# Half-row transposes, a shorter decoding, softmax sums dealt to 128 partitions and a third value buffer in a fused attention and two-MLP kernel

## The chip, the cores and the metric

One core of a Trainium2 chip runs the whole program. The metric is the device time of one execution in microseconds (us); lower is better. PE is TensorE (PEld its weight loads), DVE is VectorE, ACT is ScalarE, POOL is GpSimd and SP is SyncE, which issues most of the transfers.

## What is computed

Attention with a tanh cap over 2 batches of 12 heads (448 tokens, 64 columns per head), then an MLP with a sigmoid gate, then an MLP with RMS norm and a SiLU gate. The change touches attention alone.

```python
scores = scale * np.matmul(q, k.transpose(0, 1, 3, 2))
scores = cap * np.tanh(scores / cap)
attn = np.exp(scores - max)
attn = attn / (np.sum(attn, axis=-1, keepdims=True) + 1e-09)
return np.matmul(attn, v)
x = _moe_ref(x, w_in, w_out)                  # h * sigmoid(1.702 h) between two products
return _moe2_ref(x, w_gate, w_val, w_out, rms_g)
```

The kernel leaves out the subtraction of the maximum, since the cap bounds the scores.

## The kernel before

**Precision.** Products that need it are made of three products of halves: an operand is split into a rounded part (float32r) and the rest. Weights are split too: a weight tile of 128 x 768 is decoded from its bits by a row of ScalarE passes (`square`, `sign`, `mask`, then `high_part`) and VectorE passes (`mid`, `top`, `low`, then `low_part`).

**Attention.** The 24 heads are worked on as 12 pairs, numbered 0 to 11. A loop of 13 iterations (numbered p = 0 to 12) writes the instructions of all engines by hand, and every engine keeps the order in which they are written. Iteration p holds, for TensorE: the scores of pair p for the key chunks 1 and 2 (`scores`, L298, twelve products), the scores of the last 64 keys (`scores_last`, L308), the transposes of q and k of pair p+2 (`turn`, L251), the first scores of pair p+1 (L298, six products), the output product of pair p-1 (`outputs`, L336) and its sums of exponentials (`sums`, L368). ScalarE does the tanh and the exponential of each chunk (`exps`, L320 and L321). VectorE splits the transposes (`split_kq`, L271 and L272), adds exponentials of the chunks (`add_two` L352, `add_third` L355), copies the output product out of PSUM (L344), normalizes an older pair (`normal`: L398, L410 and L417), takes the reciprocal of the sums (L373), and does its share of decoding.

**The way of the reciprocals.** The sums of a pair stand on four partitions of a PSUM tile. For pairs 0 to 8 the reciprocal goes to DRAM (`keep_recips`, L378, 3.5 KB, named recs<-rs) and comes back spread over 128 partitions (`spread`, L383, 224 KB, named r<-recs). Both are issued by POOL, whose queue also holds the two small copies of keys for `scores_last` (L274). In iteration p POOL issues, behind those copies, `spread(p-2)` and then `keep_recips(p-1)`; `spread` waits until the DRAM tile has landed. VectorE multiplies with it in `normal(p-4)`. The last three pairs use a TensorE product (L389) in place of the way through DRAM, and its operand is the reciprocal on VectorE (L373).

**The end of attention.** In iteration 12 VectorE does `normal(8)`, the reciprocal of pair 11, `normal(10)` and then `normal(11)`. The first MLP starts with two column blocks for batch 0; between the first and the second TensorE makes the spreading product of pair 11 (L389), and the third block needs every pair of batch 1 normalized.

**PSUM.** `scores_last`, `outputs` and `sums` share two buffers, so a product waits until VectorE or ScalarE has read the one before it.

Of the kernel before, what the change touches and what calls it, by code (L numbers as in the profile page):

```python
# [18 lines left out]
def attn_moe_kernel(  # L19
# [23 lines left out]
    NC = 3  # L43
# [75 lines left out]
    def square(w):  # L119
# [5 lines left out]
        nc.scalar.activation(out=f(d), in_=f(r[:, :, 1]), func=AF.Square, scale=2.0 ** 15)  # L125
# [51 lines left out]
    def attention():  # L177
        with ExitStack() as actx:
# [15 lines left out]
            vns = [ap_.tile([128, 4, NC, D], F32, name=f"vn{i}", bufs=1) for i in range(2)]  # L194
            ves = [ap_.tile([128, 2, 2, D], F32, name=f"ve{i}", bufs=1) for i in range(2)]
# [36 lines left out]
            def load_v(g):  # L232
# [3 lines left out]
                    out=vns[g % 2][:, 0:2 * n].rearrange("p h c d -> p h (c d)"),  # L236
                    in_=v[b, h0:h0 + 2 * n, 0:NC * 128].rearrange("h (p c) d -> p h (c d)", c=NC),
                )
                for e in range(2):
                    nc.sync.dma_start(  # L240
                        out=ves[g % 2][half[e], 0:n, e], in_=rows(v, p0, n, NC * 128, S)[:, e:2 * n:2]
# [4 lines left out]
            def turn(p):  # L246
# [6 lines left out]
                if p:  # L253
                    t = ps_t.tile([128, 2, 512], F32, tag="t", name="t").rearrange("p a s -> p (a s)")
                    for c in range(2 * NC + 1):
                        flip(t[:, c * 128:(c + 1) * 128], c)
# [9 lines left out]
            def split_kq(p):  # L266
                t = turned.pop(p)
                if p:
                    x = ap_.tile([128, 2, 2 * S], F32R, tag="x", name="x")
                    xs[p] = [[x[:, a, j * S:(j + 1) * S] for j in range(2)] for a in range(2)]  # L270
                    nc.vector.tensor_copy(x[:, 0], t[:, 0:2 * S])  # L271
                    nc.vector.tensor_tensor(out=x[:, 1], in0=t[:, 0:2 * S], in1=f(x[:, 0]), op=ALU.subtract)  # L272
# [54 lines left out]
            def outputs(p, cs=range(NC + 1)):  # L327
# [5 lines left out]
                for c in cs:  # L333
                    for e in range(2):
                        w = vns[g % 2][:, 2 * i + e, c] if c < NC else ves[g % 2][:, i, e]
# [6 lines left out]
                zt[p] = zrp.tile([128, S], F32, tag="z", name="z", bufs=5)  # L342
# [99 lines left out]
            def warm_up(times):  # L442
# [6 lines left out]
                3: [(square, 0)], 4: [(sign, 0)], 5: [(mask, 0)], 6: [(square, 1)], 7: [(sign, 1)],  # L449
                8: [(mask, 1)], 9: [(high_part, 0)], 11: [(high_part, 1)],  # L450
# [3 lines left out]
                6: [(mid, 0)], 7: [(top, 0)], 8: [(low, 0)], 9: [(mid, 1)],  # L454
# [17 lines left out]
            for p in range(NPR + 1):  # L472
# [32 lines left out]
                if p >= 4:  # L505
                    normal(p - 4)
# [5 lines left out]
                if p >= 2 and p - 2 < NPR - 3:  # L512
                    spread(p - 2)
# [398 lines left out]
```

## Time and profile before

| | us |
|---|---|
| median of 3 runs (608.05 to 608.64) | 608.14 |
| the profiled execution | 608.84 |
| its span from the first to the last instruction | 607.0 |
| busy: TensorE, VectorE, ScalarE, GpSimd | 599.3, 456.5, 398.2, 71.8 |

The granted TensorE clock is full speed throughout the span. A busy TensorE says little, since the records of products that are queued behind one another run together. What a stage costs is read from the starts of the same instruction in successive iterations. The chain of waits, followed back from the last instruction, is 87% TensorE and 8% transfers; a part of attention and its end are in the hands of the transfers issued by POOL.

Attention takes the first 108 us or so of the span, the rest are the two MLPs, in which TensorE runs without a pause.

### The profile page before, as it was taken

What the parts mean: (1) busy time and instruction counts of PE and PEld (TensorE: products, weight loads), DVE (VectorE), ACT (ScalarE), POOL (GpSimd) and SP (SyncE); (2) the same over time, 40 slices, a digit from 0 to 9 for tenths busy, and PEclk for the clock granted to TensorE, in tenths of its full rate; (3) what the DMA queues carried; (4) which work ended last, traced back from release to release, by engine and by line L of the source; (5) the groups of instructions that cost most, each with busy time, mean ns of one, the idle gap of its engine ahead of it and who ended that gap; (6) DMA issues with size and microseconds to landing.
All of it is one profiled execution on the core that took longest, in us unless ns stands there. A gap on an engine that the chain in (4) does not pass through costs nothing.

```text
span 607.0 us, 8472 instructions
## 1 busy us (share of the span) xinstructions
PE 599.3 (99%) x3328; PEld 510.2 (84%) x3328; DVE 456.5 (75%) x556; ACT 398.2 (66%) x533; POOL 71.8 (12%) x95
## 2 busy tenths in 40 slices
PE   8999999999999999999999999999999999999997
PEld 5555553789988899988888888899989999999997
DVE  2889998699774635667788899995588897588842
ACT  5999998499874547777676657684555483366400
POOL 4232321000000000000032202200022200122100
PEclk9999999999999999999999999999999999999999
DMA  6676232064443332333333333433133342233012
GB/s 151 157 208 175 62 108 85 7 198 139 133 155 105 104 105 59 120 127 111 105 104 105 105 104 105 130 131 105 56 119 124 118 131 84 100 105 104 1 77 105
DMA packets 78567, 67.16 MB, mean 111 GB/s; under 512 B 29440, under 2 KB 75830, under 8 KB 78528
## 3 DMA queue, kind: packets, MB, share of 16 engines
q1 hardware_dynamic: 74064, 64.27, 34.5%
q0 software_dynamic: 3664, 2.16, 1.3%
q8 instruction: 26, 0.43, 0.3%
q10 hardware_dynamic: 800, 0.20, 0.1%
q14 instruction: 13, 0.11, 0.1%
HBM read 63.80 MB, written 2.78 MB: 110 GB/s over the span
## 4 chain that ended last, share of the span: by engine, by line
PE 87%; DMA 8%; issue 2%; DVE 1%; POOL 1%; ACT 0%; POOLq 0%; DVEq 0%
PE b L598 22%; PE b L597 22%; PE b L596 22%; PE b L806 14%; DMA recs<-rs 7%; PE s L298 2%; DMA r<-recs 2%; PE v L336 1%; PE t L251 1%; POOL r L383 1%; PE v L444 1%; PE v L308 1%; PE v L368 0%; DVE x L271 0%; DVE x L272 0%
## 5 line engine op out<-in xcount | busy, mean ns | idle before, releaser
L598 PE MATMUL b<-x,ring 128*128 128x512 f32 (+1 forms) x480 | 174.3, 363 | 0.0
L597 PE MATMUL b<-x,ring 128*128 128x512 f32 (+1 forms) x480 | 174.1, 363 | 0.0
L596 PE MATMUL b<-x,ring 128*128 128x512 f32 (+1 forms) x480 | 174.0, 362 | 0.0
L596 PEld LDWEIGHTS b<-x,ring 128*128 128x128 f32 x480 | 90.1, 188 | 10.4 <-issue 0.3
L597 PEld LDWEIGHTS b<-x,ring 128*128 128x128 f32 x480 | 90.1, 188 | 9.9
L598 PEld LDWEIGHTS b<-x,ring 128*128 128x128 f32 x480 | 90.1, 188 | 9.4
L137 DVE SCALAR_TENSOR_TENSOR dec<-raw,dec 128x768 uint32<-128x768 uint32 x68 | 69.6, 1024 | 24.7 <-ACT dec L133 23.4
L806 PE MATMUL b<-ring,uA 128*128 128x384 f32 x504 | 87.8, 334 | 0.0
L806 PEld LDWEIGHTS b<-ring,uA 128*128 128x128 f32 x504 | 87.4, 188 | 0.0
L143 DVE SCALAR_TENSOR_TENSOR dec<-raw,dec 128x768 uint32<-128x768 uint32 x68 | 73.1, 1075 | 1.1
L158 ACT ACTIVATE ring<-dec 128x768 fp32r<-128x768 f32 x68 | 56.7, 834 | 21.7 <-DVE dec L149 13.5
L163 DVE TENSOR_TENSOR ring<-dec,ring 128x768 fp32r<-128x768 f32 x68 | 66.8, 984 | 4.5 <-ACT ring L158 4.5
L598 PE MATMUL b<-g,ring 128*128 128x384 f32 (+1 forms) x192 | 70.0, 365 | 0.0
L597 PE MATMUL b<-g,ring 128*128 128x384 f32 (+1 forms) x192 | 69.9, 364 | 0.0
L596 PE MATMUL b<-g,ring 128*128 128x384 f32 (+1 forms) x192 | 69.6, 362 | 0.0
L149 DVE SCALAR_TENSOR_TENSOR dec<-raw,dec 128x768 uint32<-128x768 uint32 x68 | 64.9, 954 | 1.5
L129 ACT ACTIVATE dec<-dec,edge 128x768 f32<-128x768 f32 x68 | 63.4, 932 | 1.0
L125 ACT ACTIVATE dec<-raw 128x768 f32<-128x768 f32 x68 | 61.0, 897 | 0.6 <-DVE ring L163 0.5
L133 ACT ACTIVATE dec<-dec 128x768 f32<-128x768 f32 x68 | 57.3, 842 | 1.5
L774 POOL TENSOR_TENSOR a<-a,gg 128x512 f32<-128x512 f32 (+1 forms) x18 | 29.6, 1646 | 188.6 <-DVE gg L767 188.6
L777 ACT ACTIVATE uA<-a 128x512 fp32r<-128x512 f32 (+1 forms) x24 | 13.9, 578 | 46.3 <-POOL a L774 34.5
L628 DVE TENSOR_TENSOR g<-gg,g 128x384 fp32r<-128x384 f32 (+1 forms) x32 | 20.0, 626 | 25.9 <-ACT g L625 25.7
(104 smaller groups left out, 685.3 us busy)
## 6 DMA issues: line engine op xcount, KB each, us to landing
raw<-in_moe_w_out SPq DMA_DIRECT2D x20, 768.0 KB, 4.2
raw<-in_moe_w_in SPq DMA_DIRECT2D x16, 768.0 KB, 4.6
raw<-in_moe_w_gate SPq DMA_DIRECT2D x12, 768.0 KB, 4.2
raw<-in_moe_w_val SPq DMA_DIRECT2D x12, 768.0 KB, 4.2
raw<-in_moe_w_out SPq DMA_DIRECT2D x8, 512.0 KB, 3.8
out<-oacc SPq DMA_DIRECT2D x6, 384.0 KB, 2.3
raw<-in_moe_w_out SPq DMA_DIRECT2D x8, 256.0 KB, 3.5
r<-recs POOLq DMA_DIRECT2D x9, 224.0 KB, 7.9
```

What stands on the lines that cost most here:

```text
L125: nc.scalar.activation(out=f(d), in_=f(r[:, :, 1]), func=AF.Square, scale=2.0 ** 15)
L129: nc.scalar.activation(out=f(d), in_=f(d), func=AF.Sign, bias=edge)
L133: nc.scalar.activation(out=f(d), in_=f(d), func=AF.Relu, scale=2.0 - 2.0 ** -23)
L137: nc.vector.scalar_tensor_tensor(out=d, in0=hi, scalar=3, in1=d, op0=ALU.logical_shift_left, op1=ALU.bitwise_and)
L143: nc.vector.scalar_tensor_tensor(out=d, in0=hi, scalar=0xC0000000, in1=d, op0=ALU.bitwise_and, op1=ALU.bitwise_or)
L149: nc.vector.scalar_tensor_tensor(out=d, in0=lo, scalar=29, in1=d, op0=ALU.logical_shift_right, op1=ALU.bitwise_or)
L158: nc.scalar.activation(out=t[:, 0], in_=f(dec_t[w][0]), func=AF.Copy)
L163: nc.vector.tensor_tensor(out=t[:, 1], in0=f(d), in1=f(t[:, 0]), op=ALU.subtract)
L596: nc.tensor.matmul(out=wide(o, b), lhsT=w0, rhs=x0, start=first, stop=False)
L597: nc.tensor.matmul(out=wide(o, b), lhsT=w0, rhs=x1, start=False, stop=False)
L598: nc.tensor.matmul(out=wide(o, b), lhsT=w1, rhs=x0, start=False, stop=last)
L806: nc.tensor.matmul(out=os_[t][n][:, 0:HW], lhsT=uA[xi][:, i, tok], rhs=w[:, wi, n * HW:(n + 1) * HW], start=(i == 0 and xi == 0 and wi == ...
```

## The change

- `turn`: each of the seven transposes of 128 rows becomes two of 64 rows, one for each half of the partitions, into two PSUM banks; `split_kq` reads and writes in matching pieces of 64 columns.
- `sums`: for every pair the third chunk's exponentials are added on VectorE (`add_third` now also for pairs 6 to 11), so TensorE's eight products on that chunk go. For pairs 0 to 8 VectorE copies the sums out of PSUM in place of taking the reciprocal.
- `deal` (new): a transfer issued by POOL lays the 4 x 224 sums out as 128 x 7. `keep_recips` takes the reciprocal of the 7 columns on VectorE and stores them to DRAM. Iteration p now has `spread(p-3)`, `keep_recips(p-2)`, `normal(p-5)`, `sums(p-1)` and `deal(p-1)`. At the end iteration 10 has `normal(5)` and `normal(6)`, iteration 11 `normal(7)` and `normal(9)`, iteration 12 `normal(8)` and `normal(10)`.
- Decoding of the first two weight tiles: the ScalarE passes `square`, `sign` and `mask` become one (`size`); VectorE does `clip` and `field` in place of `mid`.
- Three value buffers in place of two.

```diff
-            vns = [ap_.tile([128, 4, NC, D], F32, name=f"vn{i}", bufs=1) for i in range(2)]
+            vns = [ap_.tile([128, 4, NC, D], F32, name=f"vn{i}", bufs=1) for i in range(3)]
...
-                        flip(t[:, c * 128:(c + 1) * 128], c)
+                        for a in range(2):
+                            nc.tensor.transpose(
+                                t[:, a, c * 64:(c + 1) * 64],
+                                raws[g % 2][half[a], c, 2 * i:2 * i + 2].rearrange("p h d -> p (h d)"),
+                                ident[half[a], half[a]],
+                            )
...
-                    nc.vector.tensor_copy(x[:, 0], t[:, 0:2 * S])
+                    flat = t[:, :, 0:S].rearrange("p a (c n) -> p a c n", n=64)
+                    high, low = [x[:, m].rearrange("p (c a n) -> p a c n", a=2, n=64) for m in range(2)]
+                    nc.vector.tensor_copy(high, flat)
...
-                for c in (1, NC) if p < NP else (1, 2, NC):
+                for c in (1, NC):
...
-                nc.vector.reciprocal(out=nr[p], in_=ps[:, 0:SH])
+                if p < NPR - 3:
+                    nc.vector.tensor_copy(nr[p], ps[:, 0:SH])
+                else:
+                    nc.vector.reciprocal(out=nr[p], in_=ps[:, 0:SH])
+
+            def deal(p):
+                rs = nr[p]
+                nr[p] = zrp.tile([128, SH // 32], F32, tag="rc", name="rc", bufs=2)
+                nc.gpsimd.dma_start(out=nr[p], in_=rs[0:128:32].rearrange("n (k c) -> n k c", k=32))
 
             def keep_recips(p):
-                rs = nr[p]
+                rc = nr[p]
+                nc.vector.reciprocal(out=rc, in_=rc)
                 nr[p] = dram.tile([4, SH], F32, tag="recs", name="recs", bufs=3)
-                nc.gpsimd.dma_start(out=nr[p], in_=rs[0:128:32])
+                nc.gpsimd.dma_start(out=nr[p].rearrange("n (k c) -> (n k) c", k=32), in_=rc)
...
-                3: [(square, 0)], 4: [(sign, 0)], 5: [(mask, 0)], 6: [(square, 1)], 7: [(sign, 1)],
-                8: [(mask, 1)], 9: [(high_part, 0)], 11: [(high_part, 1)],
+                5: [(size, 0)], 7: [(size, 1)], 9: [(high_part, 0)], 11: [(high_part, 1)],
...
-                6: [(mid, 0)], 7: [(top, 0)], 8: [(low, 0)], 9: [(mid, 1)],
+                6: [(clip, 0), (field, 0)], 7: [(top, 0)], 8: [(low, 0)], 9: [(clip, 1), (field, 1)],
...
-                if p >= 4:
+                if p >= 3 and p - 3 < NPR - 3:
+                    spread(p - 3)
+                if p >= 2 and p - 2 < NPR - 3:
+                    keep_recips(p - 2)
+                if 5 <= p < NPR - 1:
+                    normal(p - 5)
+                if NPR - 2 <= p:
                     normal(p - 4)
...
-                if p >= 2 and p - 2 < NPR - 3:
-                    spread(p - 2)
                 if p >= 1:
                     sums(p - 1)
                     if p - 1 < NPR - 3:
-                        keep_recips(p - 1)
+                        deal(p - 1)
...
-                if p < NP:
+                if p < NPR:
                     add_third(p)
```

POOL's queue, from the copies of keys in iteration 4 to those of iteration 5 and the `spread` behind them, before (kb: keys for `scores_last`; r<-recs is `spread`; recs<-rs is `keep_recips`):

```order
L274 CAST kb0_108<-x_578 64x2x64 [waits DVE_49,PE_49,Pool_49]
L274 CAST kb0_108<-x_578 64x2x64 [waits Pool_49]
L383 DMA r_606<-recs_525 128x1x448 [waits DMASW6_49]
L378 DMA recs_619<-rs_617 4x224 [waits DMASW0_49,DVE_49]
L274 CAST kb1_109<-x_666 64x2x64 [waits DVE_49,PE_49,Pool_49]
L274 CAST kb1_109<-x_666 64x2x64 [waits Pool_49]
L383 DMA r_694<-recs_619 128x1x448 [waits DMASW3_49,DMASW1_49,DMASW0_49]
```

And the same stretch after (rc<-rs is `deal`; the DRAM tile that is written, 553 and 653, is the one that the next `spread` waits for):

```order
L298 CAST kb0_110<-x_625 64x2x64 [waits DVE_49,PE_49,Pool_49]
L298 CAST kb0_110<-x_625 64x2x64 [waits Pool_49]
L416 DMA r_650<-recs_553 128x1x448 [waits DMASW6_49,DMASW0_49]
L411 DMA recs_653<-rc_566 128x7 [waits DMASW1_49,DVE_49]
L405 DMA rc_666<-rs_664 128x1x7 [waits DMASW2_49,DVE_49]
L298 CAST kb1_111<-x_721 64x2x64 [waits DVE_49,PE_49,Pool_49]
L298 CAST kb1_111<-x_721 64x2x64 [waits Pool_49]
L416 DMA r_746<-recs_653 128x1x448 [waits DMASW1_49]
```

Each iteration has a third transfer, behind the other two, and each `spread` belongs to a pair one older than before.

VectorE in iteration 10, from the copy of the output product of pair 9 (L344) on, before:

```order
L344 COPY z_1120<-v_1111 128x448 [waits PE_49]
L398 TENSOR_TENSOR z_867<-z_867,r_959 128x448 [waits DMASW7_49]
L410 CAST x0_66<-z_867 128x448 [waits DVE_49]
L417 TENSOR_TENSOR x1_67<-z_867,x0_66 128x448 [waits DVE_49]
L373 RECIPROCAL rs_1140<-v_1127 128x224 [waits DMASW4_49,PE_49]
L143 SCALAR_TENSOR_TENSOR dec_738<-raw_445,dec_738 128x768
```

And after (rc is the dealt tile of pair 8, z_844 and z_943 are pairs 5 and 6, L379 is `add_third(10)`):

```order
L368 COPY z_1210<-v_1201 128x448 [waits PE_49]
L409 RECIPROCAL rc_1157<-rc_1157 128x7 [waits DMASW5_49,DMASW1_49]
L431 TENSOR_TENSOR z_844<-z_844,r_1038 128x448 [waits DMASW4_49]
L443 CAST x0_66<-z_844 128x448 [waits DVE_49]
L450 TENSOR_TENSOR x1_67<-z_844,x0_66 128x448 [waits DVE_49]
L431 TENSOR_TENSOR z_943<-z_943,r_1138 128x448 [waits DMASW7_49]
L443 CAST x0_66<-z_943 128x448 [waits DVE_49]
L450 TENSOR_TENSOR x1_67<-z_943,x0_66 128x448 [waits DVE_49]
L400 RECIPROCAL rs_1232<-v_1223 128x224 [waits PE_49]
L379 TENSOR_TENSOR ts_1199<-ts_1199,tt_1182 128x896 [waits Activation_49]
L160 SCALAR_TENSOR_TENSOR dec_893<-raw_478,dec_893 128x768 [waits DMAHW7_49]
```

The reciprocal of 7 columns, which waits for a transfer (DMASW5 is the `deal` of pair 8), a second normalization and `add_third` have come into this stretch.

## Rows read from the trace of the kernel before

**Rows 1.** Chain that ended last: start us, us, what; the end of attention

```profile
92.54 6.29 DMA recs<-rs
98.83 0.29 issue
99.12 9.49 DMA r<-recs
...
111.97 0.61 PE b L389 x8
```

**Rows 2.** Timeline of PE, first scores of iterations 3 to 7 and 10: start, us

```profile
30.36 1.57 PE L298 MATMUL s<-x 64*128 64x448 f32 x12
...
38.31 1.58 PE L298 MATMUL s<-x 64*128 64x448 f32 x12
...
46.27 1.58 PE L298 MATMUL s<-x 64*128 64x448 f32 x12
...
54.91 1.48 PE L298 MATMUL s<-x 64*128 64x448 f32 x12
...
62.75 1.49 PE L298 MATMUL s<-x 64*128 64x448 f32 x12
...
87.46 1.48 PE L298 MATMUL s<-x 64*128 64x448 f32 x12
```

**Rows 3.** Timeline of PE's weight loads in iteration 4; [idle before <-releaser]

```profile
38.31 0.50 PEld L298 LDWEIGHTS s<-x 64*128 64x128 f32 x6 [0.36 <-issue]
...
39.81 0.50 PEld L308 LDWEIGHTS v<-x,kb 128*128 128x128 f32 x3 [0.30 <-issue]
40.33 0.89 PEld L251 LDWEIGHTS t<-ident,kq 128*128 128x128 f32 x7
```

**Rows 4.** Groups of DVE, 22 to 108 us: count | busy us, mean ns | idle

```profile
L373 DVE RECIPROCAL rs<-v 128x224 f32<-128x224 f32 x11 | 17.1, 1551 | 0.3 <-PE v L368 0.3
...
L355 DVE TENSOR_TENSOR ts<-ts,tt 128x896 f32<-128x896 f32 x5 | 5.2, 1042 | 0.1
...
L410 DVE CAST x<-z 128x448 fp32r<-128x448 f32 x9 | 3.5, 394 | 0.3
...
L137 DVE SCALAR_TENSOR_TENSOR dec<-raw,dec 128x768 uint32<-128x768 uint32 x2 | 1.8, 896 | 0.0
```

**Rows 5.** Timeline of POOL, issues of transfers and copies of keys

```profile
30.75 0.82 POOL L383 DMA_DIRECT2D r<-recs  x1
...
35.98 1.33 POOL L274 CAST kb<-x 64x128 fp32r<-64x128 f32 x2 [2.81 <-DVE x L272]
...
50.75 0.80 POOL L383 DMA_DIRECT2D r<-recs  x1 [5.47 <-DMA recs<-rs]
...
59.16 0.80 POOL L383 DMA_DIRECT2D r<-recs  x1 [5.40 <-DMA recs<-rs]
...
82.23 0.80 POOL L383 DMA_DIRECT2D r<-recs  x1 [4.23 <-DMA recs<-rs]
...
99.12 0.80 POOL L383 DMA_DIRECT2D r<-recs  x1 [6.01 <-DMA recs<-rs]
```

**Rows 6.** DMA issues, 22 to 112 us: count, KB each, median us to landing

```profile
r<-recs POOLq DMA_DIRECT2D x9, 224.0 KB, 7.9
...
recs<-rs POOLq DMA_DIRECT2D x9, 3.5 KB, 7.2
```

**Rows 7.** Timeline of DVE: the shortest reciprocal, iterations 10 to 12, and after

```profile
5.02 0.16 DVE L467 RECIPROCAL tsc<-capt 128x1 f32<-128x1 f32 x1 [3.50 <-DMA capt<-in_cap]
...
93.75 0.62 DVE L344 COPY z<-v 128x448 f32<-128x448 f32 x1 [1.90 <-PE v L336]
94.29 0.61 DVE L398 TENSOR_TENSOR z<-z,r 128x448 f32<-128x448 f32 x1
...
108.64 0.63 DVE L398 TENSOR_TENSOR z<-z,r 128x448 f32<-128x448 f32 x1 [1.45 <-DMA r<-recs]
...
110.27 1.55 DVE L373 RECIPROCAL rs<-v 128x224 f32<-128x224 f32 x1
...
113.30 0.68 DVE L405 TENSOR_TENSOR z<-z,b 128x224 f32<-128x224 f32 x2
```

More of the change, by code (lines that the diff above doesn't have):

```diff
@@ L117, in attn_moe_kernel, with open_ @@
     dec_t, done = {}, set()
-    def square(w):
+    def open_(w):
         load_to(w)
@@ L123, in square, with size, clip, field @@
         dec_t[w] = (d, r[:, :, 0], r[:, :, 1])
-        nc.scalar.activation(out=f(d), in_=f(r[:, :, 1]), func=AF.Square, scale=2.0 ** 15)
+        return dec_t[w]
+    def size(w):
+        d, lo, hi = open_(w)
+        nc.scalar.activation(out=f(d), in_=f(hi), func=AF.Abs)
+    def clip(w):
+        d = dec_t[w][0]
+        nc.vector.tensor_scalar(out=f(d), in0=f(d), scalar1=2.0 ** -15, scalar2=None, op0=ALU.max)
+    def field(w):
+        d = dec_t[w][0]
+        nc.vector.tensor_scalar(
+            out=d, in0=d, scalar1=3, scalar2=0x3FFFFFFF, op0=ALU.logical_shift_left, op1=ALU.bitwise_and
+        )
+    def square(w):
+        d, lo, hi = open_(w)
+        nc.scalar.activation(out=f(d), in_=f(hi), func=AF.Square, scale=2.0 ** 15)
     def sign(w):
@@ L191, in attention @@
             raws = [ap_.tile([128, 2 * NC + 1, 4, D], F32, name=f"kq{i}", bufs=1) for i in range(2)]
-            vns = [ap_.tile([128, 4, NC, D], F32, name=f"vn{i}", bufs=1) for i in range(2)]
-            ves = [ap_.tile([128, 2, 2, D], F32, name=f"ve{i}", bufs=1) for i in range(2)]
+            vns = [ap_.tile([128, 4, NC, D], F32, name=f"vn{i}", bufs=1) for i in range(3)]
+            ves = [ap_.tile([128, 2, 2, D], F32, name=f"ve{i}", bufs=1) for i in range(3)]
             kbs = [ap_.tile([128, 2, 128], F32R, name=f"kb{i}", bufs=1) for i in range(2)]
@@ L235, in load_v @@
                 nc.sync.dma_start(
-                    out=vns[g % 2][:, 0:2 * n].rearrange("p h c d -> p h (c d)"),
+                    out=vns[g % 3][:, 0:2 * n].rearrange("p h c d -> p h (c d)"),
                     in_=v[b, h0:h0 + 2 * n, 0:NC * 128].rearrange("h (p c) d -> p h (c d)", c=NC),
@@ L240, in load_v @@
                     nc.sync.dma_start(
-                        out=ves[g % 2][half[e], 0:n, e], in_=rows(v, p0, n, NC * 128, S)[:, e:2 * n:2]
+                        out=ves[g % 3][half[e], 0:n, e], in_=rows(v, p0, n, NC * 128, S)[:, e:2 * n:2]
                     )
@@ L253, in turn @@
                 if p:
-                    t = ps_t.tile([128, 2, 512], F32, tag="t", name="t").rearrange("p a s -> p (a s)")
+                    t = ps_t.tile([128, 2, 512], F32, tag="t", name="t")
                     for c in range(2 * NC + 1):
-                        flip(t[:, c * 128:(c + 1) * 128], c)
+                        for a in range(2):
[3 more added lines that the diff above has]
+                                ident[half[a], half[a]],
+                            )
                 else:
@@ L341, in outputs @@
                     return
-                zt[p] = zrp.tile([128, S], F32, tag="z", name="z", bufs=5)
+                zt[p] = zrp.tile([128, S], F32, tag="z", name="z", bufs=6)
                 if p < NPR - 1:
```

4 lines of the change are left out of this document (2 added, 2 removed).

## The prediction, made before the changed kernel ran

> **What bounds the kernel now.** I read the chain of waits first. In the MLPs it is TensorE without a break; the edits leave those alone, so their time moves only with their start. At the end of attention the chain leaves TensorE: it runs through POOL's transfers, the store of the reciprocals (recs) and their spreading (r), up to 108.61, and comes back by VectorE to TensorE's product L389 at 111.97 [rows 1]. So two things are to be priced: how fast attention runs, and when its last reciprocals arrive.
>
> In the middle TensorE sets the pace. The same scores start at 54.91 and 62.75: 7.84 us for an iteration in which it waits for nobody. Iterations 3 and 4 take 7.95 and 7.96 (a ScalarE decoding pass in each), iteration 5 takes 8.64, and 7 to 9 take 24.71 together, 8.24 each [rows 2].
>
> Beside it runs a loop of transfers. An r moves 224 KB and takes 7.9 us to land; recs moves 3.5 KB and still takes 7.2, since it is issued right behind an r and lands right after it [rows 6, 1]. The next r waits for that recs. So the r follow each other at the pace of their own latency: 30.75, two links of 10.0 to 50.75, one of 8.4 to 59.16, three of 7.7 to 82.23, two of 8.45 to 99.12. Each issue was released by recs [rows 5]. The last r lands at 108.6, VectorE has waited 1.45 us for it, and only then comes the reciprocal of pair 11 (110.27) that L389 needs [rows 7, 1].
>
> **The change part by part.** *Sums with add_third.* The third chunk's products made iterations 7 to 9 longer: 24.71 - 3 x 7.84 = 1.2 us go on TensorE.
>
> *ScalarE's passes and the value buffers.* What iterations 3 and 4 take over 7.84 goes with the passes (.2), and what iteration 5 takes over it goes with the earlier value load and the later mask (.8): the bound from below is that the wait stays (0), but a load that no longer waits for its buffer is ahead of need by more than the .8. With the 1.2 above iteration 10 starts 2.2 us earlier, at 85.3. One more buffer costs two memsets on POOL before TensorE's first product; they lie under the warm-up.
>
> *Transposes.* A pair of half loads starts as one: six loads of 64 rows take .50 us, as three of 128 rows do [rows 3]. So seven pairs of half loads should take about what seven whole ones take (.89), and I price them at 0. The bounds: half (-.4 per iteration), if 64 columns count for half of 128; and double (+.8, the .89 without the tail of its last load), if the two loads follow one another. The switch from whole rows to half rows moves from behind the transposes to before them, which cancels.
>
> A rule speaks against the edit. The Trainium skill ("TensorE: Matmul & The Clock Gate", section "LDWEIGHTS (loading the stationary operand)") says that a load takes as long for 32 rows as for 128, only the columns count. By that rule alone, 14 loads in place of 7, the edit costs the double bound; the row on six half loads shows that the two halves load side by side, which the section does not speak of, and I follow the row.
>
> *VectorE.* For pairs 0 to 8 the reciprocal of 1.55 us becomes a copy of 128 x 224 out of PSUM, near the .34 that one of the two L405 takes, and a reciprocal of 7 columns, between the .16 of one column and the .39 of L410; I take .2 [rows 4, 7]. That is -1.0 each. add_third comes in six times more, 1.04 each, 1.0 with the overlap of neighbours. Clip and field in place of mid (.90): a one-operand pass lies between .39 (L410, 448 columns) and .90 (L137, 768); at .6 each they add .3 to iterations 6 and 9, at .9 they add .9 [rows 4]. The strided split keeps its count of elements; I price it at 0. In iterations 6 to 9 this balances; VectorE has some 7.5 us of work in 7.84.
>
> *The loop of transfers, with a third transfer.* POOL's first r comes behind the keys of iteration 3, which end at 35.98 + 1.33 = 37.3, where it was at 30.75 [rows 5]: the loop starts 6.6 us later and has the same nine links, since each r still waits for a recs issued behind the r before it. Only the kinds of links change: one of 10.0 in place of two (the first weight tiles are in by then), two of 8.4, three of 7.5 (7.7 is their average with a decoding load in it). So the r of pair 6 is issued at 37.3 + 10.0 + 16.8 + 22.5 = 86.6 and lands 8.1 later (8.45 less the .3 from landing to issue), at 94.7. Bounds: six links of 7.7 and a landing of 7.4 give 90.9; the links of before (82.23 - 30.75) and 8.1 give 96.9.
>
> Now the new wait. The deal of a pair is issued behind an r too, and VectorE waits for it in order: in iteration 10 the reciprocal of pair 8 stands behind r(6). Queued behind it on VectorE are normal(5), normal(6), the reciprocal of pair 9 (which frees a PSUM buffer for TensorE's outputs of pair 10), add_third, decoding, and so all that leads to L389. How long a deal takes with no r ahead of it no row shows. The Trainium skill ("DMA: Bandwidth & Descriptors", section "Why a DMA increments its semaphore by 16 and not by 1") says that for transfers issued by GpSimd all 16 engines post, whatever the shape; by that the deal is done only when the r ahead of it is, and the 7.2 us of recs agree. Without it there would be no wait and the sum would be that of the first rival.
>
> *The end of attention.* Without the wait, the copy at 93.75 would start at 91.5 and VectorE would be at the reciprocal of pair 8 at 92.1; with it, at 94.7. Before, VectorE went from 94.29 to the reciprocal at 110.27 in 15.98 us, 1.45 of them waiting: 14.5 of work [rows 7]. After, the same stretch has a second normalization (1.63, from 108.64 to 110.27), two add_third (2.0) and the small reciprocal (.2): 18.35. So the last reciprocal starts at 94.7 + 18.35 = 113.05. It also needs r(8): two more links of 8.45 and 8.1 give 86.6 + 16.9 + 8.1 = 111.6, and 1.63 of normal(8) 113.2. Both say 113.2 against 110.27: **+3.0 us**. What TensorE gains before is used up by waiting at the products of pair 10 and at L389; in this stretch it has less work than VectorE. From L389 on nothing changes.
>
> The profiled execution took 608.84 (span 607.0 and 1.84 around it), which becomes 611.8; on the median of 608.14 it is **611.1**.
>
> **Rivals.** (1) *The deals are in time.* If the links are all like the fastest, r(6) lands at 90.9 and VectorE is there at 92.1: the last reciprocal starts at 110.5, +.2 us, 608.3. It decides at the landing of r(6), before or after 92. For it: the links from 59.16 to 82.23. Against: the loads of q, k, v and weights that stretched links to 8.4 and 10 are still there.
>
> (2) *Faster: half-row transposes cost half.* Then iterations 3 to 9 each lose what VectorE's 7.5 us allow, .3, together 2.1; iteration 10's copy is done at 90.0, and if r(6) has landed by then (the shortest loop of all), the last reciprocal starts at 108.4: -1.9 us, 606.2. Both conditions are needed, since VectorE's 18.35 us follow whichever is later. For it: 64 columns are half of 128. Against: loads, not columns, seem to set the pace of a transpose, and the loop starts 6.6 us late.
>
> (3) *Slower still.* Half loads one after the other add .8 to seven iterations, less what the wait for the deal hides: 92.1 + 5.6 = 97.7, the last reciprocal at 116.0, +5.8, 613.9. The skill's rule on columns is this case. A loop with all the links of before gives 96.9 + 18.35 = 115.25, +5.0, 613.1.
>
> **How the numbers follow.** The forecast, a wait of 1 to 4 us for the transfers at the end, gets .52; rival 1 .22; rival 2 .13; rival 3 .13. About .2% or 1.2 us is what a measurement of this kernel can tell from no change. Faster .13 is rival 2, the same .22 is rival 1, slower .65 the rest. The range goes from 607.6 (rival 1 with cheaper new passes on VectorE) to 614.0 (rival 3's price); it leaves out most of rival 2 and the dearest of rival 3.
>
> **What would show it.** Right: the first r at about 37.3, nine r with links of 7.4 to 10; a wait of VectorE for rc<-rs in iterations 4 to 10, the longest in iteration 10; TensorE's iterations of 7.9 or so and its stalls at the outputs of pair 10 and at L389; the last reciprocal near 113. Wrong: recs landing well before the r ahead of it, links under 7; no wait of VectorE for the dealt tile; a transpose at half or double its present price; the new passes on VectorE far from .6.

## The result, and the profile after

The changed kernel takes 611.62 us (median of 6 runs, 611.1 to 614.24) where the kernel before took 608.1 in the same session (607.68 to 608.85). The ratio is 1.0059, with a 95% interval of 1.0041 to 1.0078: **3.5 us slower**, where 3.0 was forecast. The profiled execution has a span of 610.8 us, against 607.0 before.

| us from the start of the span | before | after | difference |
|---|---|---|---|
| scores of iteration 10 begin on TensorE | 87.46 | 87.05 | -0.41 |
| VectorE's z copy of iteration 10 | 93.75 | 94.87 | +1.12 |
| reciprocal of pair 11, the last one | 110.27 | 114.00 | +3.73 |
| product that spreads it (L389, now L422) | 111.97 | 115.70 | +3.73 |
| end of the span | 607.0 | 610.8 | +3.8 |

So all of the loss is made in attention, 1.1 us of it up to the copy of iteration 10 and 2.6 in the three iterations behind it; the MLPs only start later. That is read with the timelines, which are shown by engine here, each against its group of before.

TensorE's first scores, iterations 4 to 10 (start, us), against [rows 2], and behind the last of them the scores of the last 64 keys:

```profile
37.40 1.49 PE L322 MATMUL s<-x 64*128 64x448 f32 x12
...
44.92 1.49 PE L322 MATMUL s<-x 64*128 64x448 f32 x12
...
52.44 1.49 PE L322 MATMUL s<-x 64*128 64x448 f32 x12
...
61.01 1.48 PE L322 MATMUL s<-x 64*128 64x448 f32 x12
...
69.63 1.50 PE L322 MATMUL s<-x 64*128 64x448 f32 x12
...
77.46 1.49 PE L322 MATMUL s<-x 64*128 64x448 f32 x12
...
87.05 2.53 PE L322 MATMUL s<-x 64*128 64x448 f32 x12
89.51 1.35 PE L332 MATMUL v<-x,kb 128*128 128x448 f32 x3
```

Iterations 4 and 5 take 7.52 us, better than the 7.84 that was TensorE's pace before. Then come 8.57, 8.62, 7.83 and 9.59. What TensorE had gained by 52.44 (2.5 us, since the same scores stood at 54.91) is nearly all gone by 87.05. The reason stands on VectorE, whose timeline is cut here to the small reciprocals that wait for a deal, to iteration 10 and to the last reciprocal ([idle before <-releaser]), against [rows 7]:

```profile
46.50 0.20 DVE L409 RECIPROCAL rc<-rc 128x7 f32<-128x7 f32 x1 [1.70 <-DMA rc<-rs]
...
54.82 0.20 DVE L409 RECIPROCAL rc<-rc 128x7 f32<-128x7 f32 x1 [2.50 <-DMA rc<-rs]
...
63.44 0.20 DVE L409 RECIPROCAL rc<-rc 128x7 f32<-128x7 f32 x1 [1.88 <-DMA rc<-rs]
...
86.92 0.20 DVE L409 RECIPROCAL rc<-rc 128x7 f32<-128x7 f32 x1 [0.53 <-DMA rc<-rs]
...
94.87 0.62 DVE L368 COPY z<-v 128x448 f32<-128x448 f32 x1 [2.80 <-PE v L360]
95.41 0.19 DVE L409 RECIPROCAL rc<-rc 128x7 f32<-128x7 f32 x1
...
114.00 1.55 DVE L400 RECIPROCAL rs<-v 128x224 f32<-128x224 f32 x1
```

VectorE waits for the deals of iterations 4, 5, 6 and 9, 6.6 us together. From the second half of iteration 4 on it runs behind TensorE and TensorE follows it. The chain of waits shows how the lag reaches iteration 10 (start us, us, what):

```profile
48.13 6.67 DMA rc<-rs
...
57.20 6.15 DMA rc<-rs
...
81.86 0.88 DVE dec L166
...
82.77 0.84 ACT ring L175
...
85.58 0.53 ACT tl L344
...
86.16 0.96 PE v L392 x16
87.12 2.46 PE s L322 x12
```

ScalarE's decoding pass L175 stands between two of its attention passes and waits for VectorE's L166, which is late; so its passes for pair 9 are late. One of them (`tl`, L344) reads the scores of the last 64 keys and so frees the PSUM buffer that TensorE's sums need, and they wait for it until 86.16. What that does to the clock is in the busy table by stretches:

```profile
core 0: us, PE busy (x) PEld busy (x) DVE busy (x) ACT busy (x) POOL busy (x), PEclk, DMA share, GB/s
79.50:87.00 7.50, 5.50 (x54) 2.40 (x52) 6.89 (x10) 5.12 (x7) 2.81 (x6) 1.00 0.49 121
87.00:91.00 4.00, 4.00 (x21) 2.80 (x19) 3.90 (x9) 3.93 (x5) 1.98 (x3) 0.57 0.62 177
91.00:100.00 9.00, 6.95 (x53) 3.29 (x51) 6.07 (x11) 6.87 (x8) 1.54 (x2) 1.00 0.13 37
100.00:104.40 4.40, 4.08 (x14) 1.40 (x16) 4.37 (x6) 1.30 (x2) 0.81 (x1) 0.61 0.13 22
```

PEclk is the granted clock: 0.57 and 0.61 in two stretches of 4 us, so for the greater part the 1.2 GHz level, and 2.4 GHz around them. Each follows a long wait of TensorE (2.0 us of it for ScalarE before 86.16, 2.4 for VectorE before 100.32). A long wait alone doesn't bring such a fall: in a_spread16 and a_nodeal (below) TensorE waits 2.38 us before 95.92 and 2.39 before 51.08, and the granted clock is 1.00 behind both. The scores at 87.05 took 2.53 where the six rows above them took 1.5, and those of the last 64 keys took 1.35 where they take 0.84 to 0.88 in the iterations above: 1.5 us together, all of it on the path to the copy at 94.87, and just what lies between -0.41 and +1.12 in the table. The other stretch costs little, because VectorE waits only 0.38 us for TensorE behind it. The fall of the clock is not what makes the loss: of the six executions one had a mean granted clock of 1.000, and it took 611.1 us.

Last, POOL's issues, against [rows 5]:

```profile
37.10 0.81 POOL L416 DMA_DIRECT2D r<-recs  x1 [0.51 <-DMA recs<-rc]
...
46.77 0.80 POOL L416 DMA_DIRECT2D r<-recs  x1 [2.66 <-DMA recs<-rc]
...
86.91 0.80 POOL L416 DMA_DIRECT2D r<-recs  x1 [0.55 <-DMA recs<-rc]
```

and the price of an r in the page's list of DMA issues (count, KB each, median us to landing), against [rows 6]:

```profile
r<-recs POOLq DMA_DIRECT2D x9, 224.0 KB, 7.5
```

The loop is the forecast one: first r at 37.1 (37.3 forecast), then links of 9.7, 8.1, 8.5, 7.8, 7.6 and 8.0 to the r of pair 6 at 86.9 (86.6 forecast).

Two of the later issues, at 71.24 and 78.87, show no wait for recs: the key copies ahead of them ended at 71.2 and 78.7, up to 0.3 us after the recs had landed.

Why an r is so slow stands in the posts of the 16 DMA engines, which the trace has for each transfer of POOL's queue (an engine posts when it is through with its share). For the stretch behind 78.87 (times of the first post, the 14th, and the last two):

```
issued  transfer    1st    14th   15th   16th
78.87   r<-recs     81.2   81.5   86.0   86.4
79.66   recs<-rc    81.5   81.7   86.3   86.6
81.17   rc<-rs      83.0   83.4   86.5   86.8
```

Fourteen engines are through with the r 2.6 us after its issue; two carry its 224 KB and need 7.5. The recs and the deal issued behind it are done on fourteen engines too; their last two posts come 0.2 us after one another's, right behind those of the r, so they wait for the same two. The Trainium skill ("DMA: Bandwidth & Descriptors", section "Why a DMA increments its semaphore by 16 and not by 1") has the reason: a transfer is split over the largest number of engines up to 16 that divides the slowest dimension of both of its sides. The source of r is [2, 64, 448], and 2 is what it gets; the posts agree.

### The profile page after: what moved, and what is told of

It is laid out like the page before. It is cut to its first block, busy times and chain, and to the rows that moved or that the text cites. A ratio compares the mean times of both kernels' runs of the same rounds, so it can differ in the third digit from the quotient of the medians.

```text
span 610.8 us, 8565 instructions
## 1 busy us (share of the span) xinstructions
PE 596.2 (98%) x3357; PEld 505.5 (83%) x3357; DVE 453.7 (74%) x573; ACT 395.1 (65%) x529; POOL 79.5 (13%) x106
## 4 chain that ended last, share of the span: by engine, by line
PE 85%; DVE 6%; DMA 4%; ACT 3%; issue 1%; POOL 0%; DVEq 0%; POOLq 0%
PE b L634 22%; PE b L633 22%; PE b L632 22%; PE b L842 14%; DMA recs<-rc 2%; DMA rc<-rs 2%; PE v L360 2%; ACT tt L345 1%; ACT tt L344 1%; PE s L322 1%; DVE x L450 1%; DVE rs L400 1%; DVE z L431 1%; PE v L477 1%; DVE ts L379 1%
## 5 line engine op out<-in xcount | busy, mean ns | idle before, releaser
L175 ACT ACTIVATE ring<-dec 128x768 fp32r<-128x768 f32 x68 | 56.7, 834 | 26.6 <-DVE dec L166 18.4
L166 DVE SCALAR_TENSOR_TENSOR dec<-raw,dec 128x768 uint32<-128x768 uint32 x68 | 64.9, 955 | 1.4
L146 ACT ACTIVATE dec<-dec,edge 128x768 f32<-128x768 f32 x66 | 61.5, 932 | 1.0
L142 ACT ACTIVATE dec<-raw 128x768 f32<-128x768 f32 x66 | 59.3, 898 | 0.6 <-DVE ring L180 0.5
L150 ACT ACTIVATE dec<-dec 128x768 f32<-128x768 f32 x66 | 55.6, 842 | 1.5
L734 POOL TENSOR_TENSOR sqs<-sqs,sq 128x384 f32<-128x384 f32 (+1 forms) x10 | 11.7, 1166 | 235.4 <-ACT sq L730 235.4
```

What stands on the lines that cost most here:

```text
L142: nc.scalar.activation(out=f(d), in_=f(hi), func=AF.Square, scale=2.0 ** 15)
L146: nc.scalar.activation(out=f(d), in_=f(d), func=AF.Sign, bias=edge)
L150: nc.scalar.activation(out=f(d), in_=f(d), func=AF.Relu, scale=2.0 - 2.0 ** -23)
L166: nc.vector.scalar_tensor_tensor(out=d, in0=lo, scalar=29, in1=d, op0=ALU.logical_shift_right, op1=ALU.bitwise_or)
L175: nc.scalar.activation(out=t[:, 0], in_=f(dec_t[w][0]), func=AF.Copy)
```

## The experiments

Two theories stand against each other. **Transfers:** the deals lie behind an r that two engines carry, VectorE waits for them, and that costs the time. **Work:** VectorE's longer list in the last iterations costs it, and the waits fill slack. Ratios are to the kernel before in the same session, with 95% intervals. In the session of the changed kernel it took 608.1 us; in that of a_spread16, b_spread16, b_half and a_nodeal 608.8; in that of a_dealsp, a_third6, a_spread16_n4 and a_spread16_n4_t10 608.5; and in that of the other four 610.1. Times of different sessions are compared only as closely as these agree.

### r on all engines, in both kernels

```
-                nc.gpsimd.dma_start(out=nr[p], in_=d.unsqueeze(1).to_broadcast([2, 64, S]))
+                for e in range(2):
+                    nc.gpsimd.dma_start(out=nr[p][half[e]], in_=d[e:e + 1].to_broadcast([64, S]))
```

In the changed kernel, a_spread16:

> The changed kernel with one edit: the spreading r<-recs is issued as two transfers of 64 rows instead of one of [2, 64, 448]. In the changed kernel's trace 14 of the 16 DMA engines have posted 2.4 us after an r is issued and two post 6.9 us after, so one r is carried by two engines; its rows of 64 should be dealt to all. Theory (the deals and recs are late because they lie behind an r that two engines carry): each r lands 2.5 to 3.5 us after its issue, the deals land within 4 us, VectorE's waits for rc<-rs (6.6 us in all, the 2.8 us wait for TensorE at 94.87 that follows from them) go, iterations stay at 7.5 to 7.7, the last reciprocal starts at 108.5 to 109.5 instead of 114.0: 606 to 607.2. Rival (the longer work of VectorE in the last three iterations is what costs, the waits only fill slack): the last reciprocal stays within 1 us of 114.0: 610.5 to 612.

Measured: 608.03 us (607.59 to 608.55, 10 runs), ratio 0.9984 (0.9974 to 0.9993), 3.6 us less than the changed kernel's 611.62 of the other session. Its DMA issues, 22 to 112 us (count, KB each, median us to landing), and then its timelines of TensorE (iteration 10) and VectorE:

```profile
r<-recs POOLq DMA_DIRECT2D x18, 112.0 KB, 3.1
vn<-in_v SPq DMA_DIRECT2D x4, 384.0 KB, 4.8
...
rc<-rs POOLq DMA_DIRECT2D x9, 3.5 KB, 2.9
```

```profile
83.72 1.58 PE L322 MATMUL s<-x 64*128 64x448 f32 x12
...
91.01 0.19 DVE L409 RECIPROCAL rc<-rc 128x7 f32<-128x7 f32 x1
...
109.12 1.55 DVE L400 RECIPROCAL rs<-v 128x224 f32<-128x224 f32 x1
```

An r lands in 3.1 us in place of 7.5, a deal in 2.9, and there is no wait for a deal any more. Iterations 4 to 8 take 7.52 each, and the last reciprocal starts 4.9 us earlier. The whole loss is gone with the two engines: transfers, not work, in this sense. But from the deal in iteration 10 to the last reciprocal VectorE still needs 18.1 us. The time came 0.8 us above the range that was expected, though the last reciprocal came where it was expected: the profiled execution took 607.71, 5.0 less than the 612.67 of the changed kernel's, and the expectation had taken the 4.9 off the median.

In the kernel before, b_spread16:

> The kernel before with that edit alone: r issued as two transfers of 64 rows. Theory: r lands about 3 us after its issue where it took 7 to 9.5, recs no longer lands behind it, the links of the loop are no longer 7.7 to 10 us but the pace of the iterations; VectorE's wait of 1.45 us for r at 108.6 goes, the last reciprocal comes at about 108.8 instead of 110.27: 606.0 to 607.0. Rival (TensorE's own pace sets the end and the transfer only seems last): within 0.5 us of 608.1. Rival (a spread is slow through its latency, not through its two engines): latency of r stays above 6 us and nothing changes.

Measured: 607.32 us (607.18 to 608.0, 7 runs), ratio 0.9972 (0.9961 to 0.9983). The two rivals fall (an r lands in 3.4 us), and the gain is 1.4 to 1.7 us, by the medians and by the ratio. The time is 0.3 above the theory's range; the gain is the 1.1 to 2.1 that this range meant under 608.1. The last reciprocal:

```profile
107.90 1.55 DVE L373 RECIPROCAL rs<-v 128x224 f32<-128x224 f32 x1
```

It comes 2.4 us before that of [rows 7], without a wait. TensorE's product follows only at 110.46, 1.5 us earlier than before: by then TensorE itself is busy.

### The half-row transposes alone

The kernel before with the transposes and the strided split of the change, b_half:

> The kernel before with the half-row transposes and the strided split alone. The changed kernel's trace has 14 half transposes in 0.43 us, where 7 whole ones took 0.65; an iteration is 7.52 where it was 7.84. Theory (in the kernel before the loop of transfers sets the end, TensorE does not): the iterations shorten by 0.3, iteration 10 begins near 85 instead of 87.46, but the r keep their own links, the last one lands at 107.8 to 108.6, VectorE waits about 3 us for it: 607.3 to 608.3. Rival (TensorE's pace sets the end): minus 2 to 2.7 us, 605.4 to 606.1.

Measured: 609.54 us (607.36 to 613.57, 10 runs), ratio 1.0017 (0.9992 to 1.0042): no gain, and 1.2 us above the theory's range. VectorE at the end (start, us, [idle before <-releaser]):

```profile
108.77 0.62 DVE L405 TENSOR_TENSOR z<-z,r 128x448 f32<-128x448 f32 x1 [1.75 <-DMA r<-recs]
...
110.40 1.55 DVE L380 RECIPROCAL rs<-v 128x224 f32<-128x224 f32 x1
```

The last r lands when it did, whatever TensorE does: before the change, the loop of transfers set the end. That was the theory, and the rival (a gain of 2 us or more) falls. One part of the theory is wrong: iterations 3 and 4 still take 7.96 and 7.97, since ScalarE's passes hold them, iteration 5 takes 8.96 with a wait of 1.30 for its values, and 7 to 9 take 8.0 each, so iteration 10 begins at 87.20 and not near 85. Half rows, with that r on all engines, b_half_spread16:

> The kernel before with r in two transfers of 64 rows (607.3 by itself) and the half-row transposes. Theory (TensorE has 0.31 us less per iteration, but ScalarE holds iterations 3 and 4 at 7.97, and VectorE with some 7.9 us of work holds 7 to 9): iteration 10 begins at 85.3 to 86.0 instead of 86.58, 606.2 to 607.1. Rival (the 0.31 goes through in every iteration): 604.5 to 605.6.

Measured: 606.84 us (606.65 to 607.48, 5 runs), 0.5 below b_spread16, which ran in another session and whose range overlaps with this one. In the traces TensorE's last product starts 0.4 earlier (110.03). The scores of iteration 10 begin at 86.08, and TensorE's weight loads of the sums wait for ScalarE's passes nine times (us in total, times, longest):

```profile
PEld v L375 <- ACT tl L327: 8.7, 9, 1.1
```

So with the old decoding the shorter transposes turn into waits for ScalarE. With the lighter decoding, in a_spread16, iterations 4 to 8 take 7.52; that it is the decoding alone which lets them through was not shown, since it wasn't run by itself.

### The deal taken out, and put on another queue

Without the deal, a_nodeal:

```
-                if p < NPR - 3:
-                    nc.vector.tensor_copy(nr[p], ps[:, 0:SH])
-                else:
-                    nc.vector.reciprocal(out=nr[p], in_=ps[:, 0:SH])
+                nc.vector.reciprocal(out=nr[p], in_=ps[:, 0:SH])
...
+                if p >= 4:
...
+                if p >= 2 and p - 2 < NPR - 3:
+                    spread(p - 2)
...
-                        deal(p - 1)
+                        keep_recips(p - 1)
```

> The changed kernel without the deal: reciprocals of 128x224 on VectorE, recs, r and the normalizations in the places of the kernel before; transposes, decoding, add_third and three value buffers stay. Theory (the deals' waits cost): VectorE has 1.0 us more in each of the iterations 2 to 9 and some 8.4 us of work in iterations 6 to 9, so it sets the pace there, but it waits for no transfer before the last r: last reciprocal at 110.5 to 112, 608 to 609.8. Rival (add_third for the second half is what costs): the end is as late as in the changed kernel or later, 611 to 613.

Measured: 612.26 us (610.87 to 613.42, 5 runs), ratio 1.0049 (1.0032 to 1.0065). That is not what the theory expected: without the deal the time is the same or worse, inside the rival's range. Two things show, on VectorE and on TensorE:

```profile
81.56 1.55 DVE L397 RECIPROCAL rs<-v 128x224 f32<-128x224 f32 x1
...
90.11 1.55 DVE L397 RECIPROCAL rs<-v 128x224 f32<-128x224 f32 x1
...
112.10 0.62 DVE L422 TENSOR_TENSOR z<-z,r 128x448 f32<-128x448 f32 x1 [0.67 <-DMA r<-recs]
...
51.08 2.48 PE L360 MATMUL v<-tt,vn 128*64 128x448 f32 x12 [2.39 <-DMA vn<-in_v]
```

VectorE, with the wide reciprocal and add_third both, needs 8.55 us for this iteration, with no idle time between; and the two-engine r still costs, now in a value load (51.08) and at the end (0.67). A deal thus takes a real load off VectorE. What it is worth without the slow r is the next pair: a_nodeal_spread16 against a_spread16_n4, which differ by the deal alone.

> The changed kernel without the deal and with r in two transfers of 64 rows; normalizations in iteration p+4. It differs from a_spread16_n4 (606.2) by the deal alone. Theory (with the transfers out of the way a deal is worth what it takes off VectorE, since VectorE has about 8.5 us of work per iteration from iteration 5 on without it and 7.5 with it): iterations 6 to 9 at 8.3 to 8.7, last reciprocal at 110.5 to 111.8, 608.8 to 610.5. Rival (without the deal only the slow r had cost, the 612.3 of a_nodeal is the transfer loop): 606 to 607.

Measured: 609.81 us (608.96 to 610.18, 10 runs) against the 606.2 of a_spread16_n4 (below): the deal is worth 3.6 us, and its rival falls. The two ran in different sessions: by the ratios it is 2.3 us, and in the traces, from the scores of iteration 3 to the last reciprocal, 3.4 (80.6 against 77.2). So of the 6.1 us between a_nodeal and a_spread16_n4 some 2.5 are the transfers and the rest the work that a deal takes off VectorE.

The deal issued by SP, a_dealsp:

```
-                nc.gpsimd.dma_start(out=nr[p], in_=rs[0:128:32].rearrange("n (k c) -> n k c", k=32))
+                nc.sync.dma_start(out=nr[p], in_=rs[0:128:32].rearrange("n (k c) -> n k c", k=32))
```

> The changed kernel with one edit: the deal rc<-rs is issued by SP instead of POOL; r and recs stay on POOL as they are. Theory (the deal lands late because it stands behind an r on POOL's one queue, not because the DMA engines are busy): a deal lands 2 to 3.5 us after its issue though an r is in flight, VectorE's waits for rc<-rs (6.6 us in the changed kernel) go, TensorE's iterations are 7.5 to 7.7 and iteration 10 begins at 83.5 to 85 instead of 87.05; but recs still lands behind r, the r keep links of 7.4 to 10, the last r lands at 108 to 109.5 and holds the last reciprocal at 110 to 111.5 instead of 114.0: 607.5 to 609. Rival (the DMA engines are what the deal waits for): deals land with the r ahead of them as now and the time stays at 611 to 612.

Measured: 617.77 us (616.42 to 621.62, 4 runs), ratio 1.0165 (1.0128 to 1.0201), which neither side had. SP's queue, and TensorE:

```profile
49.85 0.58 SPq L405 DMA_DIRECT2D rc<-rs  x1
50.53 2.55 SPq L252 DMA_DIRECT2D vn<-in_v  x1
...
54.98 3.97 PE L360 MATMUL v<-tt,vn 128*64 128x448 f32 x9 [6.14 <-DMA vn<-in_v]
```

VectorE waits for no deal any more, though each r still takes some 7 us, and the four iterations behind are 7.52, 7.52, 7.52 and 8.24. Of the theory a part holds. From SP a deal posts five times in place of 16. The deals issued at 71.28, 79.00, 86.51 and 94.03 have all their posts after 2.0 to 2.3 us, each with an r in flight, so the DMA engines as a whole are not full. But the deal of 38.34 has its last two posts at 44.6, right behind the r of 36.91, which landed at 44.25. That of 49.85 takes 5.5 us. So POOL's queue is not the whole cause: this fits a deal that goes over a few engines, mostly misses the two that carry the r, and otherwise waits for them from SP's queue too. And SP's queue is in order as well. The deal stands in it and waits for VectorE's copy, and the value loads that SP issues at 37.95 and 40.34 in the changed kernel go out at 47.49 and 50.53. TensorE waits 6.1 us for them, once, and the last reciprocal starts at 119.05. The expectation had left out what is queued behind the deal.

### VectorE's work

The third chunk of pairs 6 to 11 back on TensorE, a_third6:

```
-                for c in (1, NC):
+                for c in (1, NC) if p < NP else (1, 2, NC):
...
-                if p < NPR:
+                if p < NP:
                     add_third(p)
```

> The changed kernel with the third chunk of the sums of pairs 6 to 11 back on TensorE; everything else stays, the deals and the two-engine r too. Each of these pairs takes 1.0 us off VectorE and gives TensorE 0.4 us. Theory (VectorE's work after iteration 10 begins is a part of the loss, 2 x 1.0 us of the 18.6 it does there; the waits for the deals are the rest): the wait at iteration 10 stays, VectorE reaches the deal of pair 8 at 94.3 to 95.4 as before, the last reciprocal starts 2 us earlier than 114.0, at 111.5 to 112.3: 608.9 to 609.9. Rival (add_third is covered by the waits, since VectorE waits 6.6 us for deals): 611 to 612. Rival (add_third is the whole loss): 608 or less.

Measured: 614.38 us (611.76 to 614.86, 4 runs), ratio 1.009 (1.0064 to 1.0116): that is above what the theory and both rivals had. Nothing is gained, so add_third is not the whole loss. Its waits for deals (us in total, times, longest), and VectorE's reciprocal of pair 8:

```profile
DVE rc L409 <- DMA rc<-rs: 11.0, 7, 4.6
```

```profile
96.92 0.20 DVE L409 RECIPROCAL rc<-rc 128x7 f32<-128x7 f32 x1 [0.77 <-DMA rc<-rs]
```

11.0 us of waits in place of 6.6: here the loop had links of 9.4, 10.9 and 8.9 at its start, and iteration 10 waits for the deal after all, to 96.9. This run doesn't tell whether the 2 us of VectorE's work are worth something under a slow r; the loop varies by more than that from one execution to the next. That is seen in the times as well: in the sessions of the experiments kernels with the two-engine r spread over 2.5 to 6 us (before in the last session 607.59 to 612.75, b_half 607.36 to 613.57), those with r on all engines over 0.8 to 1.2 (a_spread16 607.59 to 608.55, a_spread16_n4 605.88 to 606.85).

With r fast the question has an answer. a_spread16_n4 puts the normalization of pair p into iteration p+4 throughout:

```
-                if 5 <= p < NPR - 1:
-                    normal(p - 5)
-                if NPR - 2 <= p:
+                if p >= 4:
                     normal(p - 4)
```

> The changed kernel with r in two transfers of 64 rows, and the normalization of pair p in iteration p+4 throughout (the changed kernel has it in p+5 up to iteration 9 and does two in iteration 10). Theory (with r on all engines, the time is VectorE's work from the z copy of iteration 10 on, 18.1 us from 91.01 to the last reciprocal at 109.12): the second normalization of iteration 10, 1.6 us, moves to iteration 4, where VectorE waits anyway; the last reciprocal starts at 107.3 to 107.8: 606.2 to 606.8. Rival (TensorE or the transfers hold the end): 607.5 to 608.3.

Measured: 606.2 us (7 runs), ratio 0.9963 (0.9947 to 0.9978), 1.8 less than a_spread16 of the session before (1.3 by the ratios); 1.6 was the second normalization. Then without add_third for the last two pairs, a_spread16_n4_t10 (the diff of a_third6 with NPR - 2):

> The last one, and the third chunk of pairs 10 and 11 on TensorE (sums with three chunks, no add_third). Theory: VectorE's work from iteration 10 on loses 2.0 more, 14.5 us in all; TensorE, which waits 2.75, 1.8 and 1.1 us for VectorE there, does the 0.8 us in these waits; the last reciprocal starts at 105.3 to 106.3 and the time is 604.2 to 605.4. Rival (TensorE is next to bound it): 605.4 to 606.8, no better than without.

Measured: 605.19 us (604.45 to 605.32, 4 runs), ratio 0.9945 (0.993 to 0.996). The gain is 1.0, and the time lies in the theory's range, near its upper end. The last reciprocal and TensorE's product of it:

```profile
105.76 1.55 DVE L400 RECIPROCAL rs<-v 128x224 f32<-128x224 f32 x1
...
108.34 0.61 PE L423 MATMUL b<-rs,sel 32*64 32x224 f32 x8
```

The reciprocal is where it was expected; TensorE's product comes 2.6 us behind it and without a wait. TensorE is the bound again, by its waits further up.

### A version that beats both, and the price of the transposes

a_best2 takes those waits on: ScalarE's pass L175 for tile 0 one iteration later, normalization behind the reciprocal in iteration 10, add_two of pair 11 behind the z copy.

```
-                5: [(size, 0)], 7: [(size, 1)], 9: [(high_part, 0)], 11: [(high_part, 1)],
+                5: [(size, 0)], 7: [(size, 1)], 10: [(high_part, 0)], 11: [(high_part, 1)],
...
-                    if p != 1:
+                    if p != 1 and p < NPR - 1:
                         add_two(p)
...
+                if p == NPR - 1:
+                    add_two(p)
...
-                if p >= 4:
+                if p >= 4 and p != NPR - 2:
                     normal(p - 4)
...
+                if p == NPR - 2:
+                    normal(p - 4)
```

> a_spread16_n4_t10 (605.2) with three moves in the last iterations: the high part of weight tile 0 on ScalarE in iteration 10 instead of 9 (it waits for VectorE there and TensorE for it, 1.2 and 0.7 us), the normalization of iteration 10 behind the reciprocal that frees TensorE's bank (1.1 us), add_two of pair 11 behind the z copy (0.8 us). Theory: TensorE's waits of 3.8 us between 83 and 99 fall to about 1.5, the MLP begins 1.2 to 2.5 us earlier: 602.8 to 604.1. Rival (the waits come back at the next product): 604.6 to 605.4.

Measured: 603.8 us (603.36 to 604.22, 6 runs), ratio 0.9903 (0.9885 to 0.9922) in a session in which the kernel before took 610.08; against its 608.1 to 608.8 of the other sessions it is 4.3 to 5.0 us. The same with whole-row transposes, a_best2_whole:

> The last one with the whole-row transposes and the plain split of the kernel before. With the transfers fast, TensorE sets the pace of iterations 2 to 8. Theory (half rows cost 0.43 us a pair where whole rows cost 0.65, and an entry and exit less: 0.31 per iteration): iterations of 7.83 instead of 7.52, 1.8 to 2.8 us slower than a_best2. Rival (the halves are worth nothing, as the prediction priced them): within 0.5 us of it.

Measured: 605.9 us (605.74 to 606.62, 6 runs), 2.1 more. From the timelines of TensorE, the transposes of one pair, first in a_best2_whole, then in a_best2:

```profile
56.12 0.93 PE L268 MATMUL t<-ident,kq 128*128 128x128 f32 x7
```

```profile
54.63 0.65 PE L274 MATMUL t<-ident,kq 64*128 64x64 f32 x14
```

From the first start to the last that is 0.65 and 0.43 us, the figures of the expectations: two halves start within 4 ns of each other and such pairs follow at some 62 ns, whole ones at 109. An iteration is 7.85 with whole rows and 7.52 with halves, and here, where TensorE sets the pace, the 0.33 go through: the forecast's price of 0 is wrong by that much per iteration.

## Why the prediction was right, and where it was not

**The end and its sign: right.** Last reciprocal at 114.0 (113.2 forecast), time 611.6 (611.1). VectorE needed 18.59 us from the reciprocal of pair 8 to the last one; the step had 18.35. Its pieces are the second normalization, two add_third and the small reciprocal, and a_spread16_n4 and a_spread16_n4_t10 gave the first two back: the same stretch is 18.1 in a_spread16, 16.5 and 14.5 in these two. The step had a second way to 113.2, by the r of pair 8, issued at 103.5 and landed at 111.6. That one did not come into play: the r was issued at 101.92 and had landed at 109.85, and VectorE came to it at 112.38 without a wait.

**The loop of transfers: right in times and cause.** First r, r of pair 6 (86.9 against 86.6) and its deal (94.2 against 94.7) came as forecast. The first owes something to chance: it was released by its recs, which landed at 36.81, where the step had it wait for the keys, which ended at 36.59. The rule that all 16 engines post, cited there, agrees with the posts: the deal's last two come 0.2 us behind those of recs. What the step didn't see is why an r takes 7 us; the same section of the Trainium skill has that too, and a two-line edit removes it.

**The wait for the deal: right that it is there, wrong in its place.** It was put into iteration 10, as the longest. It came in iterations 4 to 6 (1.70, 2.50, 1.88), and in iteration 10 VectorE waited for TensorE, until 94.87, when the deal had landed at 94.2. The step that failed is the comparison of deal and VectorE in one iteration only; the early iterations, in which a link of the loop is 8 to 10 us and an iteration 7.5, were not gone through. The lag that they leave goes by ScalarE's L175 to TensorE, which waits 2.0 us at 86.16 (0.63 at the same place in a_spread16, which has no such lag) and loses 1.5 by the clock, and ends within 0.7 us of the place that the deal itself would have set. So the size of the first part (+1.1 up to the copy, against some +0.4 in the sum's own terms) owes something to chance. An estimate from these rows: without the 1.5 of clock the copy would have been done at 93.9, VectorE would have waited for the deal until 94.2 as forecast, and the last reciprocal would have started 1.2 earlier, at 112.8.

**Transposes: mis-sized.** Priced at 0, with bounds of -0.4 and +0.8; measured -0.33, near the lower bound. That two half loads run side by side was right, and less than the whole of it: 14 halves take 0.65 us where 7 whole rows take 0.93. The Trainium skill's rule on loads ("TensorE: Matmul & The Clock Gate", section "LDWEIGHTS (loading the stationary operand)"), by which 14 loads would have cost double, doesn't cover this case: each load takes the same here, 0.14 us with 64 rows as with 128, but two of half the rows go side by side; the rows decide. The error didn't reach the time, because a gain on TensorE is waited away when the transfers set the end (b_half). For rival 2 this was its first condition, and it was met; its second, an r of pair 6 landed by 90, was not (93.8).

**TensorE's other gains.** Iteration 5 lost its wait for values (0.8), which the step gave to the third buffer and the shorter passes. a_nodeal has both and waits 2.39 us there. Its r are issued at 30.22 and 40.95, as before the change, and the value load beside the second, at 41.20, ends on fifteen engines by 45.1 and on the last at 50.95. In the changed kernel the first r is issued at 37.10, the value load at 37.95, and it lands at 46.8, before TensorE needs it at 48.39. So that gain came at least in part from the later first r. The passes of ScalarE were worth more than the 0.2 of the sum: they hold iterations 3 and 4 at 7.96 once the transposes are short.

**VectorE's new passes: right.** Groups of VectorE after, 24 to 116 us (count | busy us, mean ns), against [rows 4]:

```profile
L379 DVE TENSOR_TENSOR ts<-ts,tt 128x896 f32<-128x896 f32 x11 | 11.8, 1073 | 0.1
...
L295 DVE CAST x<-t 128x896 fp32r<-128x896 f32 x8 | 8.7, 1088 | 5.0 <-PE t L274 5.0
...
L398 DVE COPY rs<-v 128x224 f32<-128x224 f32 x8 | 3.0, 374 | 0.2 <-PE v L392 0.2
...
L409 DVE RECIPROCAL rc<-rc 128x7 f32<-128x7 f32 x9 | 1.8, 197 | 6.6 <-DMA rc<-rs 6.6
...
L136 DVE TENSOR_SCALAR dec<-dec 128x768 uint32<-128x768 uint32 x2 | 1.1, 560 | 0.1
L132 DVE TENSOR_SCALAR dec<-dec 128x768 f32<-128x768 f32 x2 | 1.1, 552 | 0.0
```

0.37 for the copy (0.34), 0.20 for seven columns (0.2), 0.55 and 0.56 for clip and field (0.6), 1.07 for add_third (1.0); the strided split keeps its 1.09. The lighter VectorE is what the change could have gained: with r on all engines the deal's part of it is worth some 2.3 to 3.6 us.

**Open.** Why the loop's links differ by 1 to 3 us between executions of one kernel wasn't settled; the lighter decoding and the third buffer weren't run alone.

## What to carry to other kernels

Before a small transfer is put on the critical path, look at what is ahead of it on its queue, and at how many engines carry that: a broadcast whose source has an outer dimension of 2 goes over two engines, and whatever is issued behind it and needs those two waits for them. Compare a loop of transfers with the loop of engines in every iteration and not only in the last, since a lag that arises early is passed on by whichever engine has an in-order wait. A saving on an engine is worth its size only where that engine sets the pace: half-row transposes gave 0 in one kernel, at most about 0.5 us in another and 2.1 in a third.

## What the runs showed of the hardware

Two half-row transposes, of 64 rows each, are cheaper than one of 128: 14 took 0.65 us, 7 whole ones 0.93. A two-engine transfer on POOL's queue also delays loads of SP's queue, which go over all 16 engines: the four large value loads took 7.9 us to land in the changed kernel and 4.8 with r on all engines. And in the changed kernel TensorE's waits of 2.0 and 2.4 us were each followed by some 4 us in which the granted clock was about 0.6, while waits of 2.4 us in a_spread16 and a_nodeal, and one of 3.1 in a_third6, were not.
